# Single-token attention over a 65,536-key cache: VectorE forms ScalarE's products of a quarter ahead of its own sums of the preceding quarter, and ScalarE copies the turned outputs one quarter later

## The chip, the core and the metric

The kernel runs on one core of one Trainium2 chip. The metric is the device time of one execution in microseconds (us), as the median of several runs; the profile is of one execution, and its span runs from the first to the last instruction. The engines are TensorE (PE in the profile; PEld is its weight load), VectorE (DVE), ScalarE (ACT), GpSimd (POOL) and SyncE (SP), which here issues the DMA transfers. The notes in a program such as L247 are line numbers of the kernel before.

## What is computed

One token attends to a long cache with 16 heads, and the result is scaled by a small dense block with silu. Cut to what matters:

```python
# x (1,1,448); k_cache, v_cache (1,16,65536,256); wq (448,4096); wo (4096,448); w1, w2: 448 -> 1792 -> 448; all bf16
def _A_ref(x, k_cache, v_cache, wq, wo):
    q = (x @ wq).reshape(B, Sq, H, Dh).transpose(0, 2, 1, 3)
    scores = jnp.einsum("bhqd,bhkd->bhqk", q, k_cache) * (Dh ** -0.5)
    p = _softmax(scores, axis=-1)
    o = jnp.einsum("bhqk,bhkd->bhqd", p, v_cache)
    return o.transpose(0, 2, 1, 3).reshape(B, Sq, H * Dh) @ wo

xn = _layernorm(x, axis=-1)
s = _A_ref(xn, A_k_cache, A_v_cache, A_wq, A_wo)
g = _silu(_B_ref(xn, B_w1, B_w2))
return x + s * g
```

K and V of all heads are 16 x 65,536 x 256 x 2 bytes = 537 MB each, and each element is used once.

## The kernel before

A head's 65,536 keys are cut into 4 blocks of 16,384 keys (128 partitions x 128 keys), 64 blocks in all. A block of K is 8.39 MB, and so is one of V. Three buffers `R[0..2]` of that size hold K of a block, and then, in the same place, its V.

For one block:

- VectorE multiplies K by the query, in place, in four quarters of 32 keys a partition. Of each quarter's 32 keys it leaves 18 products to ScalarE to be summed (`NA = 18`), sums 12 itself with one reduction, and does 2 with a fused multiply and sum (`MIX = (2, 12)`).
- ScalarE sums its 18 products a quarter, one activation with an accumulator for each.
- At the block's end VectorE waits for ScalarE's sums (`pf`), copies the scores, which lets SyncE load V over K (`kf`), and finds the maximum with TensorE's help. ScalarE forms the exponentials, and TensorE multiplies them by V of the block (64 matmuls), which lets SyncE load a new K (`vf`, `vh`).
- ScalarE copies the unnormalized outputs of an earlier block out of PSUM (`act_out`), TensorE turns them to a column (`pe_turn`), and ScalarE copies the column to `hist` (`act_row`).

```python
KB, SUB, NR = 128, 32, 3
MIX, MIXL = (2, 12), (6, 8)
NA = SUB - sum(MIX)                       # 18 keys of a quarter for ScalarE
...
def load_k(i, s, h=None):                 # SyncE
    if h is not None:
        take(sp, h)                       # vh: first half of V used
    take(sp, vf[s])                       # V of the buffer used
    sp.dma_start(out=R[s][:, :], in_=block(Kd, i)).then_inc(kl[s], 16)      # L205
    ...
def load_v(i, s):
    take(sp, kf[s])                       # K of the buffer used
    sp.dma_start(out=R[s][:, :], in_=block(Vd, i)).then_inc(vl[s], 16)      # L211
...
def dve_block(s, mix, between=None):      # VectorE, one block
    def end(c0, c1, own):
        take(dve, pf, (c1 - c0) // SUB)   # ScalarE's sums of these quarters
        take(dve, sd, own)
        dve.tensor_copy(out=S2[:, c0:c1], in_=S[:, c0:c1]).then_inc(kf[s], 1)   # L239
        dve.reduce_max(out=rmax[:, :], in_=S[:, c0:c1], axis=AX.X).then_inc(rm, 1)
        if c0 == 0 and between:
            between()
        dve_gmax()
    ...
    take(dve, qr)
    dve.tensor_copy(out=qcur[:, :], in_=ps_q).then_inc(sd, 1)                # L255
    ...
    take(dve, kl[s], 16)                  # K landed
    for k in range(NSTEP):                # 4 quarters
        ...
        m = times(c2, c3)                 # L247: products of 18 keys for ScalarE
        m.then_inc(mr, 1)
        times(c1, c2).then_inc(sd, 1)     # L247: products of its own 12 keys
        for c in range(c0, c1):           # L272: 2 keys, product and sum in one
            dve.tensor_tensor_reduce(...)
        ins = dve.tensor_reduce(          # L282: sums of the 12 keys
            out=S[:, c1:c2], in_=Kv[:, c1:c2, :], axis=AX.X, op=ALU.add)
        ...                               # after the last quarter (and, in the last block, after the second): end(...)

def act_sums(b, c0):                      # ScalarE, one quarter
    take(act, mr)
    for c in range(SUB - NA, SUB):        # L298
        ins = act.activation(out=prod, in_=prod, func=ACT.Identity, accum_out=S[...])
    ins.then_inc(pf, 1)

def act_out(po=psO):
    take(act, od)                         # TensorE has done an earlier block's V
    act.copy(out=O[:, :], in_=po).then_inc(oc, 1)                            # L324
def act_row(e):
    take(act, ho)                         # TensorE has turned it
    return act.copy(out=hist[...], in_=ps_t)                                 # L332

def pe_block(i, s):                       # TensorE, one block
    pe_turn()                             # waits for oc, gives ho
    pe_max(i)                             # L349, L380, L355: waits for rm
    pe_v(s)                               # V of the block before: L337 x64, gives od, vf
```

ScalarE runs a loop with a step for each quarter. After the second quarter of a block it does `act_keep`: the copy of the outputs and, right behind it, the copy of the turned column. The last block is cut in two halves with a maximum each, its mix is `MIXL = (6, 8)`, and its loads of V and of `wo` come in pieces.

Of the kernel before, what the change touches and what calls it, by code (L numbers as in the profile page):

```python
# [14 lines left out]
KB = 128  # L15
SUB = 32
NR = 3
MIX, MIXL = (2, 12), (6, 8)
NA = SUB - sum(MIX)
# [4 lines left out]
def kernel(  # L24
# [12 lines left out]
    nc = tc.nc  # L37
# [17 lines left out]
    NSTEP = KB // SUB  # L55
# [14 lines left out]
    pe, dve, act, gp, sp = nc.tensor, nc.vector, nc.scalar, nc.gpsimd, nc.sync  # L70


    KW, HK = KB * Dh, KB // 2
# [84 lines left out]
    def sem(name):  # L158
        return tc.alloc_semaphore(name)

    def take(e, s, k=1):
        e.wait_ge(s, k).then_inc(s, -k)  # L162

    kl = [sem(f"kl{t}") for t in range(NR)]
    kh = [sem(f"kh{t}") for t in range(NR)]
    kq = [sem(f"kq{t}") for t in range(NR)]
# [4 lines left out]
    mr = sem("mr")  # L171
# [4 lines left out]
    sd, sa = sem("sd"), sem("sa")  # L176
# [17 lines left out]
    def at(n):  # L194
        return slice(n, n + 1) if isinstance(n, int) else bass.ds(n, 1)
# [30 lines left out]
    def dve_gmax():  # L226
        take(dve, tm)
        dve.reduce_max(out=gmax[0:1, :], in_=ps_m[0:1, :], axis=AX.X).then_inc(gm, 1)  # L228


    def dve_block(s, mix, between=None):
        nt, nr = mix
        Kv = R[s][:, :].rearrange("p (c d) -> p c d", d=Dh)


        def end(c0, c1, own):
            take(dve, pf, (c1 - c0) // SUB)
# [7 lines that stand above are left out]
        def times(c0, c1):  # L245
            keys = Kv[:, c0:c1, :]
            return dve.tensor_tensor(  # L247
                out=keys,
                in0=keys,
                in1=qcur[:, None, :].to_broadcast([P, c1 - c0, Dh]),  # L250
                op=ALU.mult,
            )

        take(dve, qr)
        dve.tensor_copy(out=qcur[:, :], in_=ps_q).then_inc(sd, 1)  # L255
        own = 1
        halves = between is not None
        take(dve, kl[s], 16)
        for k in range(NSTEP):
            if k == 1:  # L260
                take(dve, kq[s], 16)
            if k == NSTEP // 2:
                take(dve, kh[s], 16)
            c0, c1, c2, c3 = k * SUB, k * SUB + nt, k * SUB + nt + nr, (k + 1) * SUB
            m = times(c2, c3)
            if k == 0:
                m.wait_op(sd, 1, "sem-ge")
            m.then_inc(mr, 1)
            times(c1, c2).then_inc(sd, 1)
            own += 1  # L270
            for c in range(c0, c1):
                dve.tensor_tensor_reduce(  # L272
                    out=Kv[:, c, :],
                    in0=Kv[:, c, :],
                    in1=qcur[:, :],
                    scale=1.0,
                    scalar=0.0,
                    op0=ALU.mult,
                    op1=ALU.add,
                    accum_out=S[:, c : c + 1],  # L280
                )
            ins = dve.tensor_reduce(  # L282
                out=S[:, c1:c2], in_=Kv[:, c1:c2, :], axis=AX.X, op=ALU.add
            )
            ins.wait_op(sd, own, "sem-ge")
            if k == NSTEP - 1:
                ins.then_inc(sd, 1)
                end(KB // 2 if halves else 0, KB, own + 1)
            elif halves and k == NSTEP // 2 - 1:
                ins.then_inc(sd, 1)  # L290
                end(0, KB // 2, own + 1)
                own = 0

    def act_sums(b, c0):
        take(act, mr)
        for c in range(SUB - NA, SUB):
            prod = RR[:, bass.ds(b + c * Dh, Dh)]
            ins = act.activation(  # L298
                out=prod,
                in_=prod,  # L300
                func=ACT.Identity,
                accum_out=S[:, bass.ds(c0 + c, 1)],
            )
        ins.then_inc(pf, 1)
# [17 lines left out]
    def act_out(po=psO):  # L322
        take(act, od)
        act.copy(out=O[:, :], in_=po).then_inc(oc, 1)  # L324

    def act_keep(e):
        act_out()
        return act_row(e)

    def act_row(e):  # L330
        take(act, ho)
        return act.copy(out=hist[:, at(e + 2), 2:4].rearrange("p o s -> p (o s)"), in_=ps_t)  # L332
# [120 lines left out]

    def act_steps():
        g, es, name = act, {act.engine}, f"steps_{nc.next_id()}"
        body, norm, more, keep, soft, wrap, join, out, last, l1, s2, l2, s3, l3, tail = (
            f"{name}_{x}"
            for x in "body norm more keep soft wrap join out last l1 s2 l2 s3 l3 tail".split()
        )
        ri, rb, rp, rc = (nc.alloc_registers(f"{name}_{x}", engines=es) for x in "ibpc")  # L460
        for r in (ri, rb, rp, rc):
            nc.regs_mov(r, 0)
        end = NR * KW

        def add(r, n):
            nc.regs_alu(r, r, n, op=mybir.AluOpType.add)

        def block_no():
            return nc.snap(ri, min_val=0, max_val=LAST - 1)

        nc.br(body, engines=es)
        with nc.body(body, valid_engines=es):
            act_sums(
                nc.snap(rb, min_val=0, max_val=end - SUB * Dh),
                nc.snap(rc, min_val=0, max_val=KB - SUB),
            )
            add(rb, SUB * Dh)
            add(rc, SUB)
            g.br_lt(ri, LAST, on_true=norm, on_false=last)
        with nc.body(norm, valid_engines=es):  # L480
            g.br_eq(rc, HK, on_true=keep, on_false=more)
        with nc.body(more, valid_engines=es):
            g.br_lt(rc, KB, on_true=body, on_false=soft)
        with nc.body(keep, valid_engines=es):
            act_keep(block_no() - 2)
            nc.br(body, engines=es)
        with nc.body(soft, valid_engines=es):
            p = nc.snap(rp, min_val=0, max_val=(NR - 1) * KB)
            act_softmax(block_no(), PVV[:, bass.ds(p, KB)])
            nc.regs_mov(rc, 0)  # L490
            add(ri, 1)
            add(rp, KB)
            g.br_lt(rb, end, on_true=join, on_false=wrap)
        with nc.body(wrap, valid_engines=es):
            nc.regs_mov(rb, 0)
            nc.regs_mov(rp, 0)
            nc.br(join, engines=es)
        with nc.body(join, valid_engines=es):
            g.br_lt(ri, LAST, on_true=body, on_false=out)
        with nc.body(out, valid_engines=es):  # L500
            act_out()
            nc.br(body, engines=es)
        with nc.body(last, valid_engines=es):
            g.br_eq(rc, SUB, on_true=l1, on_false=s2)
        with nc.body(l1, valid_engines=es):
            act_row(LAST - 2)
            nc.br(body, engines=es)
        with nc.body(s2, valid_engines=es):
            g.br_eq(rc, HK, on_true=l2, on_false=s3)
        with nc.body(l2, valid_engines=es):  # L510
            take(act, wx)
            act.activation(out=wgt[:, 0:N1], in_=wgt[:, 0:N1], func=ACT.Exp).then_inc(wy, 1)
            act_softmax(LAST, PV[0][:, 0:HK], 0, HK)
            nc.br(body, engines=es)
        with nc.body(s3, valid_engines=es):
            g.br_lt(rc, KB, on_true=l3, on_false=tail)
        with nc.body(l3, valid_engines=es):
            act_out()
            nc.br(body, engines=es)
        nc.switch_bb(tail)  # L520

    with tc.tile_critical():
# [8 lines left out]
            out=w2_t, in_=B_w2.rearrange("(p c) d -> p (c d)", c=FC)  # L531
# [13 lines left out]
        for T, w, b, d in ((ident[:], P, 0, -1), (eye2[:, 0, :], 2, 0, -1), (eye2[:, 1, :], 2, -1, 1)):  # L545
            mark("gp", gp.affine_select(
                out=T, in_=T, compare_op=ALU.not_equal, fill=1.0, base=b,
# [12 lines left out]
            out=rstd, in_=mv[0:1, 1:2], func=ACT.Sqrt, bias=eps_t, scale=1.0  # L560
# [5 lines left out]
            out=xn,  # L566
# [7 lines left out]
        for z in range(2):  # L574
            t5 = mark("dve", dve.tensor_copy(
                out=xz[0:1, z, :].rearrange("o (r y) -> o y r", y=2)[:, z, :],
# [5 lines left out]
        for c in range(DX):  # L582
# [13 lines left out]
            out=Z.rearrange("p (c n) -> p c n", c=DX)[:, :, 0 : (HP - 1) * (HP + 1) + 1 : HP + 1],  # L596
# [125 lines left out]


        loop(dve, 0, LAST, NR, lambda i, s: dve_block(s, MIX))
        act_steps()


# [106 lines left out]
        def keys(po, t, s, cut, sems, a, b, start, done=None):  # L834
# [45 lines left out]
            out=OT[:, :, H1],  # L880
# [17 lines left out]
            out=x_f[0:1, :], in0=g_t, in1=x_f[0:1, :], op=ALU.add  # L898
# [33 lines left out]
```

## Time and profile before

| | |
|---|---|
| median of 3 runs | 2561.09 us (2560.86 to 2561.91) |
| span of the profiled execution | 2558.6 us |
| busy share: PE, DVE, ACT | 45%, 84%, 76% |
| DMA queue 1, share of 16 engines' time | 99.1% |
| read from HBM | 1084.29 MB |

A busy share is an average over the span. The DMA line of the page shows in 40 equal slices how busy the core's 16 DMA engines were, in tenths (9 is 90% or more). In a view of waits, a row names the engine and the line that waited, then what released it ("DVEq" and "ACTq" are an engine's own queue, in which a semaphore was waited for), the total in us, how often, and the longest. In a timeline, a row has the start in us, the duration in us, engine, line, operation, out and in, and in brackets the idle time ahead of it. In the view of groups, the numbers behind the count are busy us, mean ns of one, and idle us ahead.

### The profile page before, as it was taken

To read this page: it belongs to the slowest core of one execution; us is meant where nothing else is said; L and a number is where in the kernel's file an instruction comes from. 1 tells how busy PE (TensorE), PEld (TensorE's weight loads), DVE (VectorE), ACT (ScalarE), POOL (GpSimd) and SP (SyncE) were. 2 spreads that over 40 slices of the span, in tenths; PEclk is the share of its full clock that TensorE was granted. 3 is DMA by queue.
4 is the path that set the end of the run, shared out by engine and by line. 5 is a ranking of instruction groups with operands and counts; after the bars stand their busy time and mean duration, and the time that the engine had idled before them with its cause. 6 is when DMAs were issued, how large, how long until landed. Compare 5 with 4: busy or idle time off the path is not lost. (4 is left out here: it accounts for less than half of the span.)

```text
span 2558.6 us, 30100 instructions
## 1 busy us (share of the span) xinstructions
PE 1156.8 (45%) x4738; PEld 439.7 (17%) x4738; DVE 2159.7 (84%) x2117; ACT 1949.4 (76%) x9556; POOL 1.9 (0%) x14
## 2 busy tenths in 40 slices
PE   3253453543534435435345354453443534534557
PEld 1121111211211112111111121121111211111112
DVE  6978988889889888898888888988988889889886
ACT  5877878778778787787777877877878778778785
POOL 0000000000000000000000000000000000000000
PEclk7676776767767767667676676776776767767778
DMA  9999999999999999999999999999999999999997
GB/s 419 428 438 427 427 425 426 424 423 433 424 426 421 429 430 426 425 432 420 425 426 426 425 424 419 439 425 423 429 423 427 424 415 434 426 432 428 426 422 325
DMA packets 23308, 1084.40 MB, mean 424 GB/s; under 512 B 2434, under 2 KB 4612, under 8 KB 4996
## 3 DMA queue, kind: packets, MB, share of 16 engines
q1 hardware_dynamic: 23298, 1084.30, 99.1%
q8 instruction: 4, 0.07, 0.0%
q14 instruction: 4, 0.03, 0.0%
q10 hardware_dynamic: 2, 0.00, 0.0%
HBM read 1084.29 MB, written 0.00 MB: 424 GB/s over the span
## 5 line engine op out<-in xcount | busy, mean ns | idle before, releaser
L298 ACT ACTIVATE R<-R x4608 | 1840.0, 401 | 354.3 <-ACTq L162 354.2
L247 DVE TENSOR_TENSOR R<-R,qcur 128x4608 bf16<-128x4608 bf16 (+1 forms) x512 | 1077.6, 2145 | 158.3 <-DVEq L162 158.1
L337 PE MATMUL bank<-R,PV 128*2 128x512 bf16 x4096 | 1035.6, 420 | 16.5 <-PEq L162 6.6
L298 ACT ACTIVATION_READ_ACCUMULATOR R<-R x4608 | 862.2, 187 | 0.0
L282 DVE TENSOR_REDUCE S<-R 128x12 f32<-128x3072 bf16 (+1 forms) x256 | 852.3, 3329 | 0.0
L337 PEld LDWEIGHTS bank<-R,PV 128*2 128x2 bf16 x4096 | 368.3, 91 | 655.5 <-issue 221.8
L349 PE MATMUL bank<-ident,rmax 128*1 128x128 bf16 x65 | 17.1, 263 | 1001.1 <-PEq L162 1001.1
L272 DVE CUSTOM_DVE_ANT_0 R<-R,qcur 128x256 bf16<-128x256 bf16 x528 | 200.7, 417 | 0.0
L366 PE MATMUL bank<-eye,O 2*128 2x2 f32 x264 | 39.9, 252 | 347.9 <-PEq L162 347.9
L349 PEld LDWEIGHTS bank<-ident,rmax 128*1 128x1 bf16 x65 | 5.2, 79 | 1006.0 <-issue 1006.0
L239 DVE COPY S<-S 128x128 f32<-128x128 f32 (+1 forms) x65 | 14.7, 226 | 157.5 <-DVEq L162 157.5
L311 ACT ACTIVATE hist<-bank 128x1 f32 (+1 forms) x65 | 11.1, 171 | 135.0 <-ACTq L162 135.0
L366 PEld LDWEIGHTS bank<-eye,O 2*128 2x128 f32 x264 | 36.2, 207 | 365.2 <-issue 365.2
L332 ACT COPY hist<-bank 128x2 f32 (+1 forms) x66 | 10.5, 159 | 60.2 <-ACTq L162 60.2
L324 ACT COPY O<-bank 2x512 f32<-2x512 f32 x67 | 37.4, 558 | 15.9 <-ACTq L162 15.9
L228 DVE TENSOR_REDUCE gmax<-bank 1x1 bf16<-1x128 f32 x65 | 18.3, 281 | 35.8 <-DVEq L162 35.8
L272 DVE DVE_READ_ACCUMULATOR2_ANT S<- 128x1 f32 x528 | 42.5, 80 | 0.0
L255 DVE CAST qcur<-bank 128x256 bf16<-128x256 f32 x64 | 27.2, 424 | 18.1 <-DVEq L162 18.0
L313 ACT ACTIVATE PV<-S,hist 128x128 f32 (+1 forms) x65 | 26.0, 400 | 14.7 <-ACTq L162 14.4
L380 PE MATMUL bank<-q,ident 8*128 (+1 forms) x63 | 24.3, 386 | 7.5 <-issue 1.0
L240 DVE TENSOR_REDUCE rmax<-S 128x1 bf16<-128x128 f32 (+1 forms) x65 | 18.1, 279 | 0.0
L355 PE MATMUL bank<-gmax,ones_row 1*128 1x1 bf16 x65 | 10.3, 159 | 4.6 <-PEq L162 0.6
(70 smaller groups left out, 104.5 us busy)
## 6 DMA issues: line engine op xcount, KB each, us to landing
R<-in_A_k_cache_dram SPq DMA_DIRECT2D x7, 4096.0 KB, 26.2
R<-in_A_v_cache_dram SPq DMA_DIRECT2D x6, 2048.0 KB, 21.3
R<-in_A_k_cache_dram SPq DMA_DIRECT2D x2, 2048.0 KB, 19.8
R<-in_A_wq_dram SPq DMA_DIRECT2D x1, 3072.0 KB, 12.8
R<-in_A_v_cache_dram SPq DMA_DIRECT2D x3, 1024.0 KB, 21.2
R<-in_A_wo_dram SPq DMA_DIRECT2D x2, 1120.0 KB, 18.1
R<-in_B_w_dram SPq DMA_DIRECT2D x1, 1568.0 KB, 25.1
R<-in_B_w_dram SPq DMA_DIRECT2D x1, 1344.0 KB, 5.6
```

Of the source, the lines that this page charges most:

```text
L228: dve.reduce_max(out=gmax[0:1, :], in_=ps_m[0:1, :], axis=AX.X).then_inc(gm, 1)
L247: return dve.tensor_tensor(out=keys, in0=keys, in1=qcur[:, None, :].to_broadcast([P, c1 - c0, Dh]), op=ALU.mult,)
L255: dve.tensor_copy(out=qcur[:, :], in_=ps_q).then_inc(sd, 1)
L272: dve.tensor_tensor_reduce(out=Kv[:, c, :], in0=Kv[:, c, :], in1=qcur[:, :], scale=1.0, scalar=0.0, op0=ALU.mult, op1=ALU.add, accum_out=S ...
L282: ins = dve.tensor_reduce(out=S[:, c1:c2], in_=Kv[:, c1:c2, :], axis=AX.X, op=ALU.add)
L298: ins = act.activation(out=prod, in_=prod, func=ACT.Identity, accum_out=S[:, bass.ds(c0 + c, 1)],)
L313: act.activation(out=pv_out, in_=S2[:, c0:c1], func=ACT.Exp, bias=col(0, 1), scale=scale, accum_out=col(1, 2),).then_inc(pv, 1)
L324: act.copy(out=O[:, :], in_=po).then_inc(oc, 1)
L337: ins = pe.matmul(po, lhsT=PV[t][:, c : c + 2], rhs=R[s][:, c * Dh : (c + 2) * Dh], start=(start and c == k0), stop=(stop and c == k1 - 2),)
L349: pe.matmul(ps_m[0:1, :], lhsT=rmax[:, 0:1], rhs=ident[:, :], start=True, stop=True).then_inc(tm, 1)
L366: ins = pe.matmul(ps_t2[:, 2 * a : 2 * a + 2], lhsT=Ov[:, j, a, :], rhs=eye2[:, j, :], start=(j == 0), stop=(j == 1), is_transpose=True,)
L380: pe.matmul(ps_q, lhsT=ident[0:HP, at(j)].to_broadcast([HP, P]), rhs=q8[:, o : o + Dh] if isinstance(o, int) else q8[:, bass.ds(o, Dh)], s ...
```

## The change

In VectorE's block, the products of ScalarE's 18 keys of quarter k + 1 are now formed before the reduction of quarter k, so that ScalarE finds them ready sooner; those of the first quarter are formed ahead of the loop, as before in effect. The waits for parts of K (`kq`, `kh`) move with the products.

In ScalarE's loop, the copy of the outputs stays behind the second quarter, and the copy of the turned column goes behind the third, so that TensorE has a quarter's time for the turn. The last block's steps stay as they were.

```diff
+        def landed(k):
+            if k == 1:
+                take(dve, kq[s], 16)
+            if k == NSTEP // 2:
+                take(dve, kh[s], 16)
+
+        def first(k):
+            landed(k)
+            m = times((k + 1) * SUB - NA, (k + 1) * SUB)
+            if k == 0:
+                m.wait_op(sd, 1, "sem-ge")
+            m.then_inc(mr, 1)
+
         take(dve, qr)
         dve.tensor_copy(out=qcur[:, :], in_=ps_q).then_inc(sd, 1)
         own = 1
         halves = between is not None
         take(dve, kl[s], 16)
+        first(0)
         for k in range(NSTEP):
-            if k == 1:
-                take(dve, kq[s], 16)
-            if k == NSTEP // 2:
-                take(dve, kh[s], 16)
-            c0, c1, c2, c3 = k * SUB, k * SUB + nt, k * SUB + nt + nr, (k + 1) * SUB
-            m = times(c2, c3)
-            if k == 0:
-                m.wait_op(sd, 1, "sem-ge")
-            m.then_inc(mr, 1)
+            c0, c1, c2 = k * SUB, k * SUB + nt, k * SUB + nt + nr
             times(c1, c2).then_inc(sd, 1)
             own += 1
             for c in range(c0, c1):
                 ... (fused product and sum of the 2 keys, unchanged)
+            if k + 1 < NSTEP:
+                first(k + 1)
             ins = dve.tensor_reduce(
                 out=S[:, c1:c2], in_=Kv[:, c1:c2, :], axis=AX.X, op=ALU.add
             )
... (act_keep goes)
         with nc.body(norm, valid_engines=es):
-            g.br_eq(rc, HK, on_true=keep, on_false=more)
+            g.br_eq(rc, HK, on_true=here, on_false=more)
+        with nc.body(here, valid_engines=es):
+            act_out()
+            nc.br(body, engines=es)
         with nc.body(more, valid_engines=es):
-            g.br_lt(rc, KB, on_true=body, on_false=soft)
+            g.br_eq(rc, SUB, on_true=body, on_false=three)
+        with nc.body(three, valid_engines=es):
+            g.br_lt(rc, KB, on_true=keep, on_false=soft)
         with nc.body(keep, valid_engines=es):
-            act_keep(block_no() - 2)
+            act_row(block_no() - 2)
             nc.br(body, engines=es)
```

More of the change, by code (lines that the diff above doesn't have):

```diff
@@ L324, in act_out @@
         act.copy(out=O[:, :], in_=po).then_inc(oc, 1)
-    def act_keep(e):
-        act_out()
-        return act_row(e)
     def act_row(e):
@@ L455, in act_steps @@
         g, es, name = act, {act.engine}, f"steps_{nc.next_id()}"
-        body, norm, more, keep, soft, wrap, join, out, last, l1, s2, l2, s3, l3, tail = (
+        body, norm, here, more, three, keep, soft, wrap, join, out, last, l1, s2, l2, s3, l3, tail = (
             f"{name}_{x}"
-            for x in "body norm more keep soft wrap join out last l1 s2 l2 s3 l3 tail".split()
+            for x in "body norm here more three keep soft wrap join out last l1 s2 l2 s3 l3 tail".split()
         )
```

## The prediction

> **What bounds the kernel now.** I read the page from the top: busy shares, DMA, then groups, then the view of waits, and last the timeline of one block of the loop and of the end.
>
> The page's rows on DMA:
>
> ```profile
> DMA  9999999999999999999999999999999999999997
> ...
> q1 hardware_dynamic: 23298, 1084.30, 99.1%
> ...
> HBM read 1084.29 MB, written 0.00 MB: 424 GB/s over the span
> ```
>
> VectorE is busy for 84% of the span and ScalarE for 76%, but the one DMA queue for 99.1%. Only the last of the 40 slices is below 9. A block is 8.39 MB of K and 8.39 MB of V: at 424 GB/s that is 16.78/0.424 = 39.6 us, and 64 blocks take 2533 us of the 2558.6. So the loop runs at the pace of the transfers.
>
> That share alone doesn't prove that the queue never runs dry. The views of the two load lines (first L211, V, then L205, K) give the time from issue to landing:
>
> ```profile
> DMA to landing us min/median/max: 22.7/23.9/40.7
> ...
> DMA to landing us min/median/max: 23.6/25.7/45.3
> ```
>
> One of these transfers needs 8.39/0.424 = 19.8 us by itself. So even the quickest V had 22.7 - 19.8 = 2.9 us of older work ahead of it when it was issued, the median V 4.1 us, and the quickest K 3.8 us. A load is always issued before the queue is empty. Counting packets in flight in the trace, I find 16 or more in all but a few per cent of the span; engine time without a packet adds up to about 7 us ahead of the end, scattered, and 11 us after the last load.
>
> The view of waits:
>
> ```profile
> ACT R L298 <- ACTq L162: 354.2, 188, 7.1
> DVE R L247 <- DVEq L162: 158.1, 61, 5.0
> DVE S L239 <- DVEq L162: 157.5, 65, 4.6
> ACT hist L332 <- ACTq L162: 60.2, 63, 1.0
> ```
>
> Columns: total us, times, longest. Per block VectorE waits 158.1/61 = 2.6 us ahead of its first product. The query is ready by then (its cast ended 2 us before), so this is the wait for K to land. It waits 157.5/65 = 2.4 us more at the copy of the scores, which is the wait for ScalarE's last sums. ScalarE loses 60.2/63 = 0.96 us at the row copy, waiting for TensorE to turn the output that it has just copied. The change goes at the second and third of these, and the first says that VectorE is fed by a late transfer anyway.
>
> **What the Trainium skill says.** "HBM Reference", Specifications, says that a core streaming alone gets about 425 GB/s and is bounded by its 16 DMA engines; the trace has 424 over the span, so I take this as the ceiling. "VectorE: DVE Perf Modes", the perf-mode tier table, gives a bf16 tensor_tensor two elements a cycle and tensor_reduce one. The trace agrees: 4608 elements in 2549 ns against 3072 in 3346 ns (below), twice the rate; the reduction is what ScalarE's next products stand behind now, and the longest instruction of a quarter. "Perfetto Trace Analysis", Identifying Performance Opportunities, says to improve the most-contended engine; here the change works on two others.
>
> The forms of the groups:
>
> ```profile
> L282 DVE TENSOR_REDUCE S<-R 128x12 f32<-128x3072 bf16 x252 | 843.2, 3346 | 0.0
> L247 DVE TENSOR_TENSOR R<-R,qcur 128x4608 bf16<-128x4608 bf16 x256 | 652.6, 2549 | 158.3 <-DVEq L162 158.1
> L247 DVE TENSOR_TENSOR R<-R,qcur 128x3072 bf16<-128x3072 bf16 x252 | 441.0, 1750 | 0.0
> ```
>
> **The change part by part.** Nothing is removed or added among the large instructions; only ScalarE's branches are more by one or two. I take the last block of the loop, which starts at 2457.34 us. Its quarters start on VectorE at 2457.34, 2465.44, 2473.53 and 2481.62, so 8.1 us each: 2.45 for ScalarE's products (start to start, as durations overlap a little), 1.7 for its own products, 0.7 for two fused sums, 3.27 for the reduction. Four of them end at 2489.78. ScalarE's side, and where the block ends:
>
> ```profile
> 2467.24 0.19 ACT L298 ACTIVATION_READ_ACCUMULATOR R<-R  x1
> 2468.22 0.42 ACT L298 ACTIVATE R<-R  x1 [0.79 <-ACTq L162]
> ...
> 2475.41 0.56 ACT L324 COPY O<-bank 2x512 f32<-2x512 f32 x1
> 2476.93 0.16 ACT L332 COPY hist<-bank 128x2 f32 x1 [0.96 <-ACTq L162]
> 2477.44 0.42 ACT L298 ACTIVATE R<-R  x1 [0.34 <-ACTq L162]
> ...
> 2492.16 0.23 DVE L239 COPY S<-S 128x128 f32<-128x128 f32 x1 [2.37 <-DVEq L162]
> ```
>
> Step 1, products ahead of the reduction. ScalarE needs 18 x 0.40 = 7.2 us a quarter and about 0.34 us of loop between two. Its first activation is at 2460.14, 2.8 us after VectorE's first product. It ended its first quarter at 2467.43 and then waited 0.79 us, 0.45 us more than the bare loop. With the products of quarter 1 formed at 4.84 to 7.3 us of the block, well ahead of ScalarE's need at 10.1, it starts at once. Saved: 0.45 us.
>
> Step 2, the row copy a quarter later. Between the O copy at 2475.41 and the next activation at 2477.44 lie 2.03 us; without the wait for the turn it is about 0.5 for the copy and 0.34 of loop. Saved: 1.2 us. Given back a quarter later: the row copy 0.16, its semaphore and a branch, which I put at 0.3. Net 0.9.
>
> Sum. Before, ScalarE's last sum ends some 34.6 us into the block. After: 2.8 + 4 x 7.2 + 3 x 0.34 + 0.5 + 0.3 = 33.4, so about 1.2 us less. VectorE's four quarters still take 32.4, so its 2.37 us at the copy of the scores become about 1.1. VectorE isn't the last even then, and ScalarE isn't held by its products.
>
> What that is worth in the loop. The copy of the scores frees the buffer for V, which is issued 1.2 us earlier and meets a queue with 5.3 instead of 4.1 us of backlog. K follows TensorE's V pass, which follows the same maximum: also earlier, same effect. Transfers land when they did, and VectorE's wait for K grows from 2.6 to about 3.8 us. Gain in the 63 blocks of the loop: 0.
>
> What it is worth at the end. There, work is behind the transfers:
>
> ```profile
> 2492.73 0.22 PE L349 MATMUL bank<-ident,rmax 128*1 128x128 bf16 x1 [1.28 <-PEq L162]
> ...
> 2499.00 0.57 ACT L324 COPY O<-bank 2x512 f32<-2x512 f32 x1 [4.21 <-ACTq L162]
> ...
> 2543.09 7.91 PE L337 MATMUL bank<-R,PV 128*2 128x512 bf16 x32
> ```
>
> The last loads land by about 2547, and the stretch of TensorE that starts at 2543.09 ends at 2551.0, followed by the turn, the projection and two VectorE operations. Back from there: TensorE's projections, the second maximum (2536), ScalarE's 36 sums (2520.8 to 2535.7), the first maximum (2514.4), ScalarE's first 36 sums from 2499.49, held by the O copy at 2499.00, which waits for TensorE's last 16 matmuls of an older V, which stand behind the maximum at 2492.73. TensorE waited 1.28 us for that maximum. So if the block ends 1.2 us earlier, this whole chain moves up by 1.2 us, and by no more than 1.28. The last block itself is held by ScalarE in both halves (36 x 0.40 = 14.4 us each), and the new order doesn't start either of them sooner: the first waits for the O copy, the second for the first half's maximum. The new order puts 2.45 us of the third quarter's products ahead of the first half's end on VectorE: 2 x 7.88 + 2.45 = 18.2 us from 2492.6 is 2510.8, still ahead of ScalarE's 2512.6.
>
> So the sum is 0 in the loop, 0 in the start (the first blocks load with a full queue), and -1.2 us at the end: 2561.1 - 1.2 = 2559.9.
>
> **Rivals.** (a) The queue gains from more backlog. The 7 us of scattered missing packets could be engines that ran dry while others lagged; another 1.2 us ahead of them would take a part away. Against it: all 16 must finish a load, and the slowest was not the idle one. If half came back, 2556.5. (b) The loop isn't limited by the transfers but by the cycle through VectorE and ScalarE; then 1.2 us in each of 63 blocks would save 76 us, 2485. The 2.6 us in which VectorE waits for K in nearly every block, and the minimum of 2.9 us of backlog, speak against it; it would also ask for 437 GB/s. (c) The new order costs: products laid ahead delay the reduction, ScalarE's extra branch is slower than I think, or the last block's first half becomes VectorE's. The loop has 2.6 us of slack a block for that, so only the end could lose, 1 to 2 us: 2562.
>
> **Range and chances.** The three runs before span 1.1 us. I centre on 2559.9. Below, rival (a) weighs more than anything else, so 2557.0; above, the end gaining nothing plus scatter, so 2562.0. Two per cent is 51 us: only (b) reaches it, or a stall that no view shows. Faster 0.01, same 0.98, slower 0.01.
>
> **What would show it.** Right: DMA share near 99% and 424 GB/s; the wait at the copy of the scores from 157.5 to 60-90 us; the wait at the row copy from 60.2 to near none; the wait at the first product up from 158 to 210-250 us; VectorE's and ScalarE's busy time unchanged; issue to landing longer by about 1 us; the end after the last load shorter by about 1 us. Wrong: a wait at the copy of the scores that stays above 2 us (ScalarE held by something else), or a span that moves by more than 5 us with the loads at the same rate, which would mean that the loop's bound is not where I put it.

## The result and the profile after

The changed kernel takes 2516.4 us (2516.2 to 2516.9) against 2561.5 us (2560.9 to 2562.0) for the kernel before in the same measurement: a ratio of 0.9824, 95% interval 0.9807 to 0.9841. That is 45 us less, where 1.2 us less was predicted.

The page's row of what the DMA engines moved in each of 40 slices, which the prediction didn't show, is the first thing that differs. Before:

```profile
GB/s 419 428 438 427 427 425 426 424 423 433 424 426 421 429 430 426 425 432 420 425 426 426 425 424 419 439 425 423 429 423 427 424 415 434 426 432 428 426 422 325
```

After, with the other rows on DMA:

```profile
DMA  9999999999999999999999999999999999999998
GB/s 423 425 438 434 434 434 434 434 434 432 434 434 433 433 433 434 434 434 433 433 434 433 434 434 434 434 434 434 434 434 434 434 434 434 434 434 434 434 429 364
...
q1 hardware_dynamic: 23298, 1084.30, 99.8%
...
HBM read 1084.29 MB, written 0.00 MB: 431 GB/s over the span
```

Before, the rate wanders between 415 and 439 GB/s ahead of the last slice. After, it stands at 433 or 434 in slice after slice. The same bytes are moved, and both kernels call the queue over 99% busy.

The waits after (total us, times, longest):

```profile
ACT R L306 <- ACTq L162: 378.8, 64, 10.9
DVE R L247 <- DVEq L162: 257.9, 61, 8.9
...
DVE S L239 <- DVEq L162: 6.9, 3, 3.7
```

The wait at the copy of the scores (L239) is gone from all but three blocks, and the wait at the row copy is no longer listed. VectorE waits 258 us for K instead of 158. VectorE's busy time is what it was (2159.9 us, 2159.7 before); ScalarE's is 1% lower (1930.3 us, 1949.4 before). From issue to landing, V and then K:

```profile
DMA to landing us min/median/max: 24.2/24.8/39.2
...
DMA to landing us min/median/max: 25.7/26.6/45.4
```

The minimum of V rose by 1.5 us, the median by 0.9 only.

The block of the loop that corresponds to the one in the prediction, from the timelines of VectorE and ScalarE:

```profile
2421.11 4.23 DVE L247 TENSOR_TENSOR R<-R,qcur 128x4608 bf16<-128x4608 bf16 x2 [4.45 <-DVEq L162]
...
2453.70 0.23 DVE L239 COPY S<-S 128x128 f32<-128x128 f32 x1
```

```profile
2423.90 0.42 ACT L306 ACTIVATE R<-R  x1 [6.47 <-ACTq L162]
...
2438.27 0.56 ACT L332 COPY O<-bank 2x512 f32<-2x512 f32 x1
2445.93 0.13 ACT L336 COPY hist<-bank 128x2 f32 x1
```

From the first product to the copy of the scores it is 32.6 us, where it was 34.8. ScalarE has no idle time in the block once it has started.

**Where the 45 us are.** By the trace's packets, the last input landed 2547.2 us into the span before and 2509.1 after: 38.1 us. The rest of the span, after that landing, fell from 11.4 to 5.8 us.

For the first part I looked at single packets. A full load has rows of 65,536 bytes, each one packet, and the trace has its time. The median is 2.418 us before and 2.422 after, so the DMA engines are no faster. But before, 6.9% of these packets took over 3% longer than that (up to 4.1 us), after, 0.04%. The long ones come right behind the issues of V. So I counted, for every issue in the loop, the bytes issued earlier and not yet moved (packets in flight in proportion), divided by 16 x 65,536 bytes in 2.418 us = 433.7 GB/s. I call this the work left at the issue. And I counted what was lost around the issue: the time by which packets took longer than their size at that rate asks for, plus the time in which an engine had no packet, summed over the 16 engines and divided by 16.

| kernel | work left at V's issue, min / median, us | lost at V's issues in all, us | at K's |
|---|---|---|---|
| before | 0.5 / 2.1 | 35.2 | 2.9 |
| changed | 3.4 / 3.8 | 1.0 | 1.0 |

Of the 38.1 us, 34.2 (35.2 less 1.0, at V's issues) and 1.9 (at K's) are here. The theory to test: **a load that is issued with less than about 3 us of older work left makes the queue stumble, although the queue is not empty.** The change is worth 36 us in the loop since it takes V's issue from one side of that distance to the other. The rivals: (order) the new order of VectorE's instructions by itself disturbs the transfers less; (chain) the loop is paced by the chain through VectorE and ScalarE, and got faster as that got shorter.

### The profile page after: what moved, and what is told of

It is laid out like the page before. It is cut to its first block, busy times and chain, and to the rows that moved or that the text cites. A ratio compares the mean times of both kernels' runs of the same rounds, so it can differ in the third digit from the quotient of the medians.

```text
span 2514.9 us, 30289 instructions
## 1 busy us (share of the span) xinstructions
PE 1153.9 (46%) x4738; PEld 438.4 (17%) x4738; DVE 2159.9 (86%) x2117; ACT 1930.3 (77%) x9556; POOL 1.9 (0%) x14
## 3 DMA queue, kind: packets, MB, share of 16 engines
q1 hardware_dynamic: 23298, 1084.30, 99.8%
## 5 line engine op out<-in xcount | busy, mean ns | idle before, releaser
L247 DVE TENSOR_TENSOR R<-R,qcur 128x4608 bf16<-128x4608 bf16 (+1 forms) x512 | 1093.8, 2147 | 258.0 <-DVEq L162 257.9
L319 ACT ACTIVATE hist<-bank 128x1 f32 (+1 forms) x65 | 11.1, 171 | 146.7 <-ACTq L162 146.7
L321 ACT ACTIVATE PV<-S,hist 128x128 f32 (+1 forms) x65 | 26.0, 400 | 14.7 <-ACTq L162 14.4
L239 DVE COPY S<-S 128x128 f32<-128x128 f32 (+1 forms) x65 | 14.7, 226 | 15.9 <-DVEq L162 6.9
L240 DVE TENSOR_REDUCE rmax<-S 128x1 bf16<-128x128 f32 (+1 forms) x65 | 18.2, 279 | 0.0
L321 ACT ACTIVATION_READ_ACCUMULATOR PV<-S,hist (+1 forms) x65 | 12.1, 186 | 0.0
```

What stands on the lines that cost most here:

```text
L247: return dve.tensor_tensor(out=keys, in0=keys, in1=qcur[:, None, :].to_broadcast([P, c1 - c0, Dh]), op=ALU.mult,)
L321: act.activation(out=pv_out, in_=S2[:, c0:c1], func=ACT.Exp, bias=col(0, 1), scale=scale, accum_out=col(1, 2),).then_inc(pv, 1)
```

## Experiments

The first expectations say "4.8 us" for the distance, since I first counted packets in flight as wholly left; counted in proportion it is 3 us. Ratios are to the kernel before in the same measurement.

**1. Products ahead alone.** The changed kernel with the row copy back behind the output copy:

```diff
-            g.br_eq(rc, HK, on_true=here, on_false=more)
+            g.br_eq(rc, HK, on_true=keep, on_false=more)
... (here and three go)
-            g.br_eq(rc, SUB, on_true=body, on_false=three)
+            g.br_lt(rc, KB, on_true=body, on_false=soft)
...
-            act_row(block_no() - 2)
+            act_keep(block_no() - 2)      # act_out and act_row
```

> Products ahead, the row copy left behind the output copy. Late-load theory (a V load that is issued with less than about 4.8 us of older transfers left makes the DMA engines stumble; before it was a median of 3.0 us, after 5.0): ScalarE keeps about 1.1 of the 2.2 us that a block became shorter, so V is issued with about 4 us left and part of the stumbling stays: 2522 to 2538 us. Rival, the order of VectorE's instructions itself lets the transfers run faster: all of the gain, 2516. Rival, the loop is paced by the chain through VectorE and ScalarE: half of the gain, about 2538.

Measured: 2522.5 us, ratio 0.986 (0.983 to 0.989). The wait at the copy of the scores:

```profile
DVE S L239 <- DVEq L162: 96.1, 64, 3.7
```

So 1.5 us a block is left of the 2.4. V's issue has a median of 3.3 us of work left, and 50 of 57 lie between 3.0 and 3.5. The loss is 5.2 us in all, and nearly all of it in the six issues below 3 us. Just past the distance is enough. The time is at the late-load theory's edge, and far from the chain's 2538.

**2. Row copy later alone.** The kernel before with ScalarE's new loop (the second half of the change's diff).

> Row copy a quarter later, products in the old order. ScalarE then waits for VectorE's products of the last quarter instead (they are ready at 26.8 us of the block), so the block gets only about 0.3 us shorter. Late-load theory: 2552 to 2558 us. Order of VectorE's instructions: no gain, 2561. Chain: 0.3 us x 63 = 19 us less, about 2542.

Measured: 2554.8 us, ratio 0.9975 (0.9966 to 0.9983).

```profile
DVE S L239 <- DVEq L162: 140.3, 65, 2.9
```

It takes 17 us off that wait in all, 0.26 a block, because ScalarE is then held by the products. Work left: median 2.3 us; loss 31.1 us. Both parts alone, 38 and 6 us, come to nearly the whole of 45.

**3. The old order, with V released earlier.** V in two halves; the first is released by the reduction of the third quarter:

```diff
 def load_v(i, s):
-    take(sp, kf[s])
-    sp.dma_start(out=R[s][:, :], in_=block(Vd, i)).then_inc(vl[s], 16)
+    for k0, k1 in ((0, HK), (HK, KB)):
+        take(sp, kf[s])
+        load_keys(R[s], block(Vd, i), k0, k1, vl[s])
...
+            if not halves and k == NSTEP // 2:
+                take(dve, pf, NSTEP // 2)
             ins = dve.tensor_reduce(...)
+            if not halves and k == NSTEP // 2:
+                ins.then_inc(kf[s], 1)
```

> The kernel before, with V loaded in two halves; the first half is released by the reduction of the third quarter, some 10 us earlier, the second as before. The order of instructions and the length of the chain (34.8 us) stay. Late-load theory: the queue always has more than 4.8 us ahead, the transfers run at 433 GB/s or more, 2515 to 2525 us. Order of instructions: 2561. Chain: 2561.

Measured: 2529.4 us, ratio 0.987 (0.985 to 0.990). The wait at the copy of the scores (here L240) is the old one:

```profile
DVE S L240 <- DVEq L162: 156.8, 65, 5.3
```

Both halves are issued with at least 11.1 us of work left, and the loss at V's issues falls from 35.2 to 2.9 us, with the old order and the old chain. Both rivals expected 2561. The time is above the expected range for two reasons that the expectation had not allowed for. The last input lands at 2514.6 us, 5.5 us after the changed kernel's 2509.1, about what half packets cost (see experiment 7). And the end after that takes 14.4 us here.

**4. Only V's halves, not the early release.** As 3, but both halves wait for the release that V had before. This is the control for 3.

> The kernel before with V loaded in two halves, both released where V was before; so only the size of the packets (32 KB in place of 64 KB) differs from it, and only the early release from the run with halves. Late-load theory with a distance counted in us: the distance at V's issue stays near 2.1 us, the loss stays, and half packets cost some 6 us more: 2555 to 2575 us. If the distance counts in packets of an engine, half of 3 us would be enough: 2525 to 2540 us. If the halves alone, and not the early release, made the gain: 2529 us.

Measured: 2565.9 us, ratio 1.0018 (1.0009 to 1.0027). The loss is back: 37.8 us, with a median of 2.3 us left. So in 3 it was the early release and not the halves. Only V's own packets are half as long here: the work left at V's issue is that of K, in 64 KB packets as before. So this run doesn't show whether the distance counts in us or in packets.

**5. The changed kernel, with V's release later.** The release moves from the copy of the scores to a memset behind the maximum; nothing but V's load waits for it. First with 32 elements (0.09 us):

```diff
-            dve.tensor_copy(out=S2[:, c0:c1], in_=S[:, c0:c1]).then_inc(kf[s], 1)
+            dve.tensor_copy(out=S2[:, c0:c1], in_=S[:, c0:c1])
...
             dve_gmax()
+            dve.memset(late[:, 0:32], 0.0).then_inc(kf[s], 1)
```

> The changed kernel, but V's release comes from a tiny memset behind the maximum, about 1.1 us later than the copy of the scores; nothing else is later. Late-load theory: V is issued with about 3.9 us left, and the stumbling comes back in part: 2522 to 2545 us. Order of instructions: no change, 2516. Chain: VectorE has over 4 us of slack a block, so no change by itself, 2516.

Measured: 2519.2 us, ratio 0.984 (0.981 to 0.986), below what the theory expected. The work left fell only to 3.3 us, still past the distance; the four issues between 2.5 and 3 us lost 0.24 us each, the 53 between 3 and 3.5 us lost 0.02. Then with 1024 elements, a memset of 0.91 us:

> The changed kernel with V's release behind one memset of 1024 elements a partition instead of 32 (some 0.4 to 1.0 us later than the run with the tiny one, which had a median of 3.3 us of older transfers left at V's issue). Late-load theory: 2.3 to 2.9 us left, so from the losses per load seen before (0.34 to 0.55 us each at that distance) 2535 to 2550 us. Order of instructions: no change, 2516 to 2520. Chain through VectorE: it still has over 3 us of slack, 2516 to 2520.

Measured: 2551.7 us, ratio 0.9967 (0.9954 to 0.9979), just above what the theory expected. Another 0.82 us of delay in V's issue alone costs 32 us. The work left is 2.3 us, the loss 36.5 us, and the rate wanders again as it did before the change:

```profile
GB/s 420 411 442 427 422 429 428 428 423 429 425 427 426 428 424 424 423 434 429 425 423 424 432 430 421 433 427 432 426 415 442 424 419 427 422 427 418 433 421 364
```

```profile
DVE R L249 <- DVEq L163: 258.5, 61, 9.2
```

VectorE still has all its slack, 258.5 us of waiting for K as in the changed kernel, and its order of instructions is the new one. So neither order nor chain is what the time follows. This run falsifies both rivals from the other side. A still longer delay was not measured.

**6. The same with V in halves from that late release.**

> The changed kernel with V's release behind the memset of 1024 elements, and V in two halves from that same release. Distance in us (some 2.3 us left at V's issue): 2545 to 2565 us. Distance in packets: 2520 to 2535 us.

Measured: 2557.4 us, ratio 0.9988 (0.9981 to 0.9996). A median of 2.3 us left, loss 33.5 us. So halving the packets of the load that is issued leaves the loss as it was. The expectation took this for a test of whether the distance counts in us or in packets, but as in 4 the work ahead of V is a K in 64 KB packets.

Run 3 has the other case: there K is issued behind the halves of V, in 32 KB packets. Eleven of its K's had 2.5 to 3.0 us left and lost only 0.05 us each (that is, of the 8 us after the issue, what the bytes moved in them don't need at 433.7 GB/s), where V behind 64 KB packets lost 0.2 to 0.5 us at that distance. In run 4, though, five K's behind halves lost 0.16 us each with 3.2 to 3.5 us left. So 3 us is the distance for V behind a K in 64 KB packets, and whether it depends on the packets ahead is not shown.

**7. The changed kernel with early halves.** Would still more distance help?

> The changed kernel, V in two halves with the first released some 8 us earlier. Late-load theory: the loop already runs at the full rate (losses of 2 us in all at the loads of the loop), so nothing is left to gain: 2513 to 2520 us. If the earlier issue had a worth of its own beyond the distance of 3 us: below 2510.

Measured: 2520.9 us, ratio 0.985 (0.983 to 0.986), just above the range for no gain. The first halves have at least 9.5 us of work left and lose 1.6 us in all: no gain beyond the distance. Its 32 KB packets have a mean of 1.217 us, twice which is 2.434 against 2.422 for the 64 KB ones of the changed kernel. By my estimate that costs 6 us, for the 7936 more pairs over 16 engines. The last input lands 4.0 us later than in the changed kernel.

All issues of V where the old work ran into the new, by the work left. In each cell: how many, and the mean loss in us (first halves for the two split kernels).

| work left, us | before | products ahead | row later | late, 32 | late, 1024 | old, split | late, split |
|---|---|---|---|---|---|---|---|
| under 1.5 | 9: 1.24 | 1: 0.71 | 5: 1.03 | | 7: 1.16 | 3: 0.88 | 2: 1.07 |
| 1.5 to 2 | 12: 0.70 | 1: 0.60 | 12: 0.91 | | 11: 0.78 | 12: 0.91 | 12: 0.84 |
| 2 to 2.5 | 21: 0.55 | 1: 1.14 | 19: 0.46 | | 20: 0.68 | 27: 0.65 | 21: 0.69 |
| 2.5 to 3 | 10: 0.34 | 3: 0.50 | 16: 0.36 | 4: 0.24 | 14: 0.41 | 12: 0.54 | 17: 0.35 |
| 3 to 3.5 | 4: 0.16 | 50: 0.02 | 4: 0.09 | 53: 0.02 | 4: 0.09 | 2: 0.10 | 4: 0.17 |

Seven kernels with either order, two sizes of V's packets and different chains give nearly the same curve below 3 us. The work ahead of V is a K in 64 KB packets in all of them.

## Why the prediction was wrong, step by step

**"I take this as the ceiling" (424 GB/s): wrong.** 424 was the mean of a rate that was being disturbed. A better bound stood in the trace before: a median packet of 65,536 bytes in 2.418 us on each of 16 engines is 433.7 GB/s, and one slice reached 439. The figure of about 425 GB/s that the prediction takes from the Trainium skill ("HBM Reference", Specifications) isn't the ceiling here either, as the changed kernel stands at 433 to 434 in slice after slice. 2.3% of headroom lay there, 58 us over the span, in a queue that was called 99.1% busy: a packet that takes 3.3 us instead of 2.4 counts as busy.

**"A load is always issued before the queue is empty": right in words, wrong in size, and this is the step that failed.** I took the time from issue to landing less the transfer's own time as older work: at least 2.9 us, median 4.1. Counted from packets it was at least 0.5 and in the median 2.1. The difference, some 2 us, is delay that each load has anyway between its issue and its landing, and I booked it as a cushion. And I took any cushion above zero as enough, where the runs show that V needs about 3 us here.

**"Gain in the 63 blocks of the loop: 0": wrong, 36 us.** It follows from the two steps above. The direction of the working was right: V's issue did come earlier, K's too (the median of its work left rose from 4.4 to 5.5 us), and VectorE's wait for K did grow (to 258 us; 210 to 250 was expected).

**Rival (a) was the right family with the wrong size.** I gave more backlog at most the 7 us of missing packets. The trace before also had packets that were too long, 30 us in all over 16 engines, and I had not looked at their lengths. For the argument against it, that "the slowest was not the idle one", I had measured nothing.

**The shortening of a block: 2.2 us instead of 1.2.** Between two quarters I charged ScalarE 0.34 us of loop. In the changed kernel it isn't paid: 72 sums and both copies run from 2423.90 to 2453.25, 29.35 us against 72 x 0.40 = 28.8 for the sums alone. The row copy, for which I put 0.3, adds about 0.04. So ScalarE ends ahead of VectorE, and VectorE's four quarters set the block's end, with no wait left instead of 1.1 us.

**The end: 5.6 us instead of 1.2, by another mechanism.** From the next-to-last block's copy of the scores to the end of the span it is 61.2 us after and 66.4 before. The differences lie in four stretches of TensorE. Its view of windows, before and then after (us, busy and count, granted clock, DMA share, GB/s):

```profile
2493.60:2499.00 5.40, 5.40 (x20) 0.69 0.97 407
2514.80:2519.80 5.00, 5.00 (x19) 0.73 1.00 426
2539.40:2543.10 3.70, 3.70 (x12) 0.50 1.01 389
2543.10:2551.00 7.90, 7.90 (x34) 0.89 0.25 92
```

```profile
2455.10:2458.70 3.60, 3.60 (x19) 1.00 0.93 401
2474.60:2478.30 3.70, 3.68 (x18) 1.00 1.01 430
2498.00:2499.90 1.90, 1.90 (x12) 1.00 1.03 431
2499.90:2507.30 7.40, 7.21 (x33) 1.00 0.96 371
```

The same work takes about 5.4 us less at the full granted clock. In the profiles of all six kernels with the products ahead the end after the last landing is 5.7 to 7.5 us, in those of the four without 11.1 to 14.4 us. So the short end goes with the new order of the products; why the clock stays up in these stretches was not tried.

**What stays open.** Why V needs 3 us of older work was not tried. The runs show the distance, and that it doesn't depend on the size of the issued load's own packets; for the packets ahead of it this is open. The work left is also a mean over 16 engines, and whether it is the engine with the least work that counts was not tried.

## What to carry to other kernels

A DMA queue that is 99% busy can still be slowed: compare the rate with the median packet's own rate, and look at whether the rate per slice is flat. For each load, count the work that is left when it is issued; issue to landing less the transfer's own time overstates it by the load's fixed delay. Here an instruction off the critical path that frees a buffer 2.2 us sooner is worth 36 us, since it freed the buffer for the next transfer in time, and where there is enough distance already, an earlier issue gains nothing that was seen (experiment 7).

## What the runs showed of the hardware that I had not expected

- A load of V that is issued with 1.5 to 2 us of work left ahead of it on the same queue (a K in 64 KB packets) loses 0.6 to 0.9 us of the queue's time, with 2.5 to 3 us left 0.2 to 0.5, and with 3 to 3.5 us left 0.02 where nearly all issues lie there. Having 9 to 13 us left (experiments 3 and 7) makes it no better than that.
- The loss shows mostly as longer packets (up to 4.1 us instead of 2.42), which a busy share counts as busy: 99.1% before, 99.8% after.
- ScalarE's loop over quarters, two register additions and a few branches, costs nothing that can be seen in the changed kernel's block, where ScalarE waits only ahead of the first quarter. In the kernel before it cost 0.34 us right behind the row copy that had waited for the turn.
